# Gate tiles dealt out, logits one group later, 96 rows straight from the second layer: one change to an attention and mixture-of-experts kernel

## The chip, the cores and the metric

The kernel runs as one program on one core of a Trainium2 chip. The metric is the device time of one execution in microseconds (us), the median of several. PE (TensorE) multiplies matrices, DVE (VectorE) and ACT (ScalarE) compute elementwise, POOL (GpSimd) does both and issues indirect DMAs, SP (SyncE) issues most DMAs. "SPq" and "ACTq" in a row are the DMA queues behind SP and ACT.

## What is computed

Three stages follow one another. Attention with a bias from cumulated positive scores, on 4 x 8 heads of 576 positions and width 64:

```
scores = q k^T / 8;  cum = cumsum(max(s, 0))
scores = where(causal, -1e9, scores + min(cum_j - cum_i, 0))
x = softmax(scores) v              # as 2304 tokens x 512
h = x @ w_in                       # 512 -> 2048, float64 weights
g = h * clip(h + 3, 0, 6) / 6
x = g @ w_out                      # 2048 -> 512
logits = x @ w_gate                # 8 experts, each takes 288 tokens
for (token, e) in descending order of logits:
    assign token to e, if the token is free and e not full
out[tokens of e] = max(x[tokens of e] @ w1[e], 0) @ w2[e]    # 512 -> 1024 -> 512
```

## The kernel before

**Numbers.** Every large operand is held as two 16-bit halves (high and low), and a product is three matmuls: high by high, high by low, low by high. "Split product" below is one with the low half of its left side.

**Attention.** Pairs of heads go through three stages, in a pipeline: rows of scores, columns of scores, value products. For pair n, `prep(n)` puts q and k side by side as 16-bit halves (`kq`), and line 250 turns them by a transposing DMA into `kqT`, from which line 282 takes the scores (`sc`). For pair 0 the turn is in two parts, 4 of 9 blocks on SP and 5 on ACT; for all others it is one on SP.

**First MLP.** A decoder (`decode`, lines 500 to 512, ACT, DVE and POOL) turns the float64 weights into halves, `wih`/`wil` for w_in and `woh`/`wol` for w_out (tile `W`, the low half made by POOL at line 512); `ST["w"]` counts the loads that are decoded, 8 of w_in and then 8 of w_out, two blocks of 128 rows each. Tokens go in 9 groups of 256. `h_step` (line 551) makes two blocks of h of a group (12 matmuls of 256 columns each), g is formed by ACT, DVE (559, 571) and POOL (572). `x2_tile` (lines 593 to 595) makes the MLP's output for 128 tokens, three matmuls of 512 columns for each of 16 blocks, into a bank called "mm" of which there are two; the result `xo` is stored to DRAM (`x2d`, line 620) as two halves.

**Gate and logits.** For the first ten of 18 token tiles (groups 0 to 4) the logits come straight from x2: xo is turned by DMA (`x2T`, line 608) and multiplied by the gate (`direct_logits`). For the last eight tiles (groups 5 to 8, `DEFER`) the logits are needed before x2 is there, and come from g instead: `gates` turns the 16 blocks of w_out, high and low (`gate_turn`, line 521, two DMAs from SP per block into a buffer `wT` of which there are three), multiplies them by the gate (`gate_product`, lines 527 and 528, eight matmuls per block) to `gm`, and `logits(u)` (580, 581) takes the logits of group u as 64 small matmuls of g with gm, in an "mm" bank. For groups 5 to 8 x2 follows after all logits, in the tiles 10 to 17, beside the routing.

**Routing.** The logits give a key per token and expert (`keys`); `route(ph)` finds one expert after another by a search for its threshold (compares on DVE, counts on PE, a few values passed between them, `kst` being one), and `tail` turns the selection into 288 indices. `gather` fetches the tokens' rows from x2d (POOL, line 1115, `xg`), three DMAs of 96 rows; `tokens` turns them to `xt` (line 1123, three transposing DMAs on SP). The last two token tiles are not in DRAM when the first expert's rows are gathered; they are picked out by matmuls (`pick`, line 1220) and added to xt by DVE (1223, four additions).

**Experts.** `groups(ph)` makes `ht` (first layer, line 1132, 8 blocks of 128 rows, 288 columns) and `yt` (second layer, 4 blocks, 96 matmuls in all, 288 columns). yt stands with the features down the partitions, so `store` turns it back by matmuls with the identity (line 1163, 8 for each 96 rows), copies it (ACT, 1166) and scatters the rows to the output (POOL, line 1168).

**What sets the order.** The attention, the decoder, the MLP and the gate are Python generators (`Stream`) which a planner, `merge`, deals out: it picks the stream that is least far along, each yield giving an estimate of the time its matmuls take; a yielded condition blocks a stream until it holds, and a yielded negative number -n keeps a stream back until the planner's clock has gone n ns further (the gate's stream goes first whenever it is ready). The tile framework then schedules the instructions by priority within their dependencies, adds the semaphores, and gives buffers in turn; `high_priority` lifts a block ahead of what stands near it, and `issue_after` holds a DMA behind a given instruction. Each engine runs its own instructions in the order that comes out.

Of the kernel before, what the change touches and what calls it, by code (L numbers as in the profile page):

```python
# [23 lines left out]
HP = 20000  # L24
# [75 lines left out]
def tile_attention_moe(ctx, tc, q, k, v, s, w_in, w_out, w_gate, w1, w2, out):  # L100
# [129 lines left out]
    def prep(n):  # L230
# [18 lines left out]
        for eng, s0, s1 in ((nc.sync, 0, 9),) if n else ((nc.sync, 0, 4), (nc.scalar, 4, 9)):  # L249
            pin(eng.dma_start_transpose(out=t[:, s0:s1].rearrange("p s w x -> p (s w) x"),  # L250
                                        in_=kq[:, s0:s1].rearrange("p s w x -> p (s w x)")))
# [323 lines left out]
    def logits(u):  # L575
        p = psum.tile([128, 2, 16], F32, name="mm", tag="mm", bufs=2)
        for t in range(2):
            for f in range(FT1):
# [5 lines left out]
                                axis=AX.X, op=OP.add)  # L584

    def x2_tile(t):
        u, o = divmod(t * 128, UN)
        p = psum.tile([128, DM], F32, name="mm", tag="mm", bufs=2)
        for f in range(FT1):
            if ST["w"] < 2 * FP:  # L590
                yield from wait(lambda: ST["w"] > FP + f // 2)
# [37 lines left out]
    def mlp():  # L629
        for u in range(NU):  # L630
# [4 lines left out]
            for fp in range(HE + HX if u == 1 else 0, FP):  # L635
                yield from wait(lambda: ST["w"] > fp)
                yield from h_step(u, fp)
                if fp == FP // 2 and ("x2T", 2 * u - 1) in GT:
                    direct_logits(2 * u - 1)
                    yield 8 * 27.0  # L640
                    if "keys" in GT:
                        GT["keys"](u - 1)
            if late:
                yield -2500.0
# [15 lines left out]
            yield from wait(lambda: ST["g"])  # L660
            yield from logits(u)
            if "keys" in GT:
                GT["keys"](u)
# [16 lines left out]
    def gates():  # L680
        turned = []
        for f in range(FT1 + 2):
# [5 lines left out]
            yield -2500.0  # L688
# [438 lines left out]
    def split_product(wh, wl, x, o, kt):  # L1127
        n, last = 0, 3 * kt - 1
        p = mm_tile([128, CAP])
# [9 lines left out]
    def groups(ph):  # L1139
# [9 lines left out]
        yt = [ffn.tile([128, 2, CAP], F16, name="yt", bufs=2 * KC) for _ in range(KC)]  # L1149
        YT[ph] = yt  # L1150
        for d in range(KC):
            p = split_product(w2h, w2l, lambda hl, f: ht[:, hl, f, :], d, FMT)
            e = nc.scalar.activation(yt[d][:, 0], p, AF.Copy)  # L1153
            nc.vector.tensor_tensor(yt[d][:, 1], p, yt[d][:, 0], op=OP.subtract)
            yield e.ins

    def store(ph):
        yt = YT.pop(ph)
        for j in range(3):
# [7 lines left out]
            nc.gpsimd.memset(spacer, 0.0)  # L1167
            st_ = nc.gpsimd.indirect_dma_start(out, bass.IndirectOffsetOnAxis(ap=IDX[ph][:, j:j + 1], axis=0), yo, None)  # L1168
            for o in SCAT:
                tc.declare_no_dep(st_.ins, o.ins, reason="different rows")  # L1170
            SCAT.append(st_)

    for t in range(NT - DEFER, NT):
        merge([Stream(x2_tile(t), 1.0)])
# [28 lines left out]
    for i in range(4):  # L1203
        for c in range(4):
            convert(0, i, c, GT["xo", NT - DEFER + 3 + i])
        sp = load(1, i - 1, sp) if i else load(0, 3, sp)
    g_stack.close()
    ffn = ctx.enter_context(tc.tile_pool(name="ffn", bufs=1))
    with tc.high_priority(offset=HP):
        sp = tokens(0, sp)  # L1210
# [31 lines left out]
    store(E8 - 1)  # L1242
# [28 lines left out]
```

## Time and profile before

| | |
|---|---|
| median of 3 runs | 926.36 us (924.86 to 927.57) |
| the profiled execution | 926.86 us |
| its span, first to last instruction | 924.7 us |
| PE busy | 824.6 us (89% of the span) |
| weight loads of PE (beside its matmuls) | 588.6 us (64%) |
| DVE, POOL, ACT busy | 554.3, 467.4, 373.3 us |
| mean granted clock of PE | 0.958 of full speed |

The page gives each engine's busy time for the whole span and for 40 equal slices of it. The timeline lists an engine's instructions in order of time; a wait is the idle time of an engine just ahead of an instruction, with the instruction or DMA that came last of those it needed. [...] In the timeline of the kernel before, the first h product comes at 119 us; from there to 440 us attention, h and x2 of the groups run side by side. The gate's tiles stand between 448 and 500 us, the logits and h of groups 5 to 8 between 502 and 583, x2 of the last tiles and the search for the first experts until some 685, the experts' products behind that, with the rest of the search beside them.

### The profile page before, as it was taken

The numbers are of one execution on the slowest core, as the hardware profiler recorded it, in microseconds if no ns is written. First come the engines' busy times: TensorE is split into PE (matmuls) and PEld (weight loads), VectorE is DVE, ScalarE is ACT, GpSimd is POOL, SyncE is SP. The second block draws the span as 40 slices with busy tenths as digits, with TensorE's granted clock in tenths as the row PEclk, the third lists the DMA queues.
The fourth block names the chain that finished last, engine by engine and source line by source line (L and its number), as shares of the span: only waits on it lengthen the run. The fifth ranks groups of instructions, "written<-read, shape, count | busy, mean of one in ns | idle before, by whom it ended". The sixth has DMA issues, their size and how long they took to land. (4 is left out here: it accounts for less than half of the span.)

```text
span 924.7 us, 21475 instructions
## 1 busy us (share of the span) xinstructions
PE 824.6 (89%) x8561; PEld 588.6 (64%) x8561; DVE 554.3 (60%) x1698; ACT 373.3 (40%) x704; POOL 467.4 (51%) x485
## 2 busy tenths in 40 slices
PE   1576779778899999999888999999989999999996
PEld 0354557545567857759567988444457777778885
DVE  5979879967535645513625455675777887772211
ACT  1666766656425444443111222002223554355641
POOL 1455766854433544644412433003437786787951
PEclk9976789999799999999998999999999999999998
DMA  6987999667723445221473000032346775776820
GB/s 150 213 186 186 230 184 268 134 148 182 145 52 70 96 103 102 42 51 40 89 122 57 2 1 1 13 125 104 129 129 180 189 216 167 208 214 205 194 77 26
DMA packets 225700, 116.31 MB, mean 126 GB/s; under 512 B 202272, under 2 KB 202272, under 8 KB 225600
## 3 DMA queue, kind: packets, MB, share of 16 engines
q1 hardware_dynamic: 220576, 105.01, 48.1%
q0 software_dynamic: 3072, 9.44, 3.2%
q8 instruction: 67, 1.10, 0.5%
q10 hardware_dynamic: 1952, 0.49, 0.3%
q14 instruction: 33, 0.27, 0.1%
HBM read 69.30 MB, written 9.96 MB: 86 GB/s over the span
## 5 line engine op out<-in xcount | busy, mean ns | idle before, releaser
L551 PE MATMUL mm<-xT,W 128*128 128x256 f16 (+3 forms) x2304 | 205.3, 248 | 5.4 <-DVE g L559 3.8
L1110 POOL TENSOR_TENSOR W<-stg,W 128x512 bf16<-128x512 f32 x128 | 144.7, 1157 | 92.6 <-ACT W L1108 91.8
L551 PEld LDWEIGHTS <-W 128*128 128x128 f16 (+1 forms) x2304 | 177.3, 99 | 19.2 <-issue 4.8
L1132 PEld LDWEIGHTS <-W 128*128 128x128 f16 (+1 forms) x1536 | 144.2, 98 | 38.8 <-issue 4.0
L365 POOL TENSOR_TENSOR eh<-e,eh 128x512 f16<-128x512 f32 (+1 forms) x100 | 104.6, 1061 | 102.0 <-ACT eh L363 95.2
L572 POOL TENSOR_TENSOR g<-g,g 128x512 f16<-128x512 f32 x72 | 85.3, 1185 | 134.7 <-DVE g L571 119.2
L282 PE MATMUL sc<-kqT 96*128 96x64 f16 (+10 forms) x480 | 102.1, 295 | 40.3 <-DMA kqT<-kq 22.4
L594 PE MATMUL mm<-W,g 128*128 128x512 bf16 x288 | 110.4, 383 | 6.4 <-POOL W L512 6.3
L593 PE MATMUL mm<-W,g 128*128 128x512 f16 x288 | 110.0, 385 | 5.7 <-DVE g L559 4.2
L595 PE MATMUL mm<-W,g 128*128 128x512 f16 x288 | 110.9, 385 | 0.0
L1132 PE MATMUL mm<-xt,W 128*128 128x288 f16 x768 | 103.0, 286 | 2.6 <-DVE ht L1146 2.2
L1132 PE MATMUL mm<-ht,W 128*128 128x288 f16 x768 | 102.7, 286 | 0.0
L557 ACT ACTIVATE r<-mm,three 128x512 f32<-128x512 f32 x72 | 49.4, 686 | 128.3 <-PE mm L551 123.0
L282 PEld LDWEIGHTS <-kqT 101*128 101x128 f16 (+5 forms) x768 | 52.9, 107 | 72.2 <-DMA kqT<-kq 26.4
L296 DVE TENSOR_REDUCE mx<-sc 128x1 f32<-128x384 f32 (+2 forms) x144 | 70.1, 512 | 40.3 <-PE sc L293 26.0
L362 ACT ACTIVATE e<-sc 128x512 f32<-128x512 f32 (+1 forms) x112 | 59.0, 538 | 56.2 <-PE sc L350 50.7
L559 DVE SCALAR_TENSOR_TENSOR g<-r,mm 128x512 f32<-128x512 f32 x72 | 49.2, 684 | 48.8 <-ACT r L557 48.2
L1108 ACT ACTIVATE W<-stg 128x512 f16<-128x512 f32 x128 | 75.5, 622 | 0.0
L363 ACT ACTIVATE eh<-e 128x512 f16<-128x512 f32 (+1 forms) x112 | 60.7, 570 | 22.1 <-PE pv L419 20.2
L417 PE MATMUL pv<-v,eh 128*128 128x65 f16 (+1 forms) x480 | 67.7, 203 | 1.9 <-DVE x L430 1.9
L419 PE MATMUL pv<-v,eh 128*128 128x65 f16 (+1 forms) x480 | 66.5, 199 | 2.0 <-POOL eh L365 2.0
L418 PE MATMUL pv<-v,eh 128*128 128x64 f16 (+1 forms) x480 | 66.9, 201 | 1.0 <-DVE v L220 1.0
(221 smaller groups left out, 1343.3 us busy)
## 6 DMA issues: line engine op xcount, KB each, us to landing
stg<-in_moe_w_dram SPq DMA_DIRECT2D x32, 1024.0 KB
raw<-in_moe_w_in_dram SPq DMA_DIRECT2D x8, 1024.0 KB
raw<-in_moe_w_out_dram SPq DMA_DIRECT2D x8, 1024.0 KB
x2d<-xo SPq DMA_DIRECT2D x18, 256.0 KB
ldq<-in_q_dram SPq DMA_DIRECT2D x32, 128.0 KB
ldk<-in_k_dram SPq DMA_DIRECT2D x32, 128.0 KB
ldv<-in_v_dram SPq DMA_DIRECT2D x32, 128.0 KB
ldq<-in_q_dram SPq DMA_DIRECT2D x16, 32.0 KB
```

Of the source, the lines that this page charges most:

```text
L282: nc.tensor.matmul(o, x[0:kq], y[0:kq], start=start, stop=stop)
L296: nc.vector.tensor_reduce(o, x, axis=AX.X, op=OP.max)
L365: eng.tensor_tensor(t[:, 1], e, t[:, 0], op=OP.subtract)
L417: nc.tensor.matmul(oj[:, 0:65], e[0], vv[:, 0:65], start=a, stop=False)
L551: nc.tensor.matmul(p[:, f, at:at + w], wsl(wt, ft)[:, c * 128:(c + 1) * 128], XT[b][:, c, hl, i:i + w], start=(n == 0), stop=(n == 3 * KC ...
L572: nc.gpsimd.tensor_tensor(g[:, 1].rearrange("p f x -> p (f x)"), g32, g[:, 0].rearrange("p f x -> p (f x)"), op=OP.subtract)
L593: nc.tensor.matmul(p, g[:, 0], wsl(woh, f), start=(f == 0), stop=False)
L594: nc.tensor.matmul(p, g[:, 0], wsl(wol, f), start=False, stop=False)
L595: nc.tensor.matmul(p, g[:, 1], wsl(woh, f), start=False, stop=(f == FT1 - 1))
L1108: nc.scalar.activation(h, x, AF.Copy)
L1110: nc.gpsimd.tensor_tensor(l, x, h, op=OP.subtract)
L1132: nc.tensor.matmul(p, wt[:, c, o * 128:(o + 1) * 128], x(hl, c), start=(n == 0), stop=(n == last))
```

## The change

Seven edits stand in one diff.

1. The second part of pair 0's transpose is issued by SP (`nc.sync`) instead of ACT.
2. `x2_tile` waits, while w_out is being decoded, until one load more is counted (at most all but one) before the planner may deal out the three matmuls of a block.
3. `gates` yields -4000 instead of -2500 between blocks: the planner keeps the stream back longer.
4. `logits(u)` is no longer made right after group u's h: the group's number goes into a list, `owed`, and the oldest of the list is taken within the h of a later group (after the block pairs 2 and 5 of groups 7 and 8, if one is owed and the gate is done), the rest at the end, behind the first two steps of x2 of tile 10 (`GT["begun"]`).
5. The logits are summed in a bank of the tag "tp" (name `lgp`) instead of "mm". `keys(u)` is called from `logits`.
6. `tokens(0)`, the three transposes of the first expert's rows, is called in the loop that loads and converts the first weights, ahead of the load of the second expert's third block, instead of after the loop.
7. For the last expert the second layer's product is made as before for 192 of the 288 columns only (`w`). The last 96 rows come from `store_last`: ht of these rows as the left side, w2 as the right, 24 matmuls of 512 columns, so that the result stands with the tokens down the partitions and needs no turning back. `store` of the first 192 rows is placed behind the ninth of these matmuls. `store` itself is cut in two (`put` is its scatter).

The core of the diff:

```diff
@@ prep(n)
-        for eng, s0, s1 in ((nc.sync, 0, 9),) if n else ((nc.sync, 0, 4), (nc.scalar, 4, 9)):
+        for eng, s0, s1 in ((nc.sync, 0, 9),) if n else ((nc.sync, 0, 4), (nc.sync, 4, 9)):
@@ logits(u)
-        p = psum.tile([128, 2, 16], F32, name="mm", tag="mm", bufs=2)
+        p = psum.tile([128, 2, 16], F32, name="lgp", tag="tp", bufs=TPB)
...
+        if "keys" in GT:
+            GT["keys"](u)
@@ x2_tile(t)
-                yield from wait(lambda: ST["w"] > FP + f // 2)
+                yield from wait(lambda: ST["w"] > min(FP + f // 2 + 1, 2 * FP - 1))
@@ mlp()
+        owed = []
         for u in range(NU):
...
+                if u > NU - DEFER // 2 + 1 and fp % 3 == 2 and owed:
+                    yield from wait(lambda: ST["g"])
+                    yield from logits(owed.pop(0))
             if late:
-                yield -2500.0
+                owed.append(u)
...
-            yield from wait(lambda: ST["g"])
-            yield from logits(u)
-            if "keys" in GT:
-                GT["keys"](u)
+        GT["begun"] = x2_tile(NT - DEFER)
+        for _ in range(2):
+            yield next(GT["begun"])
+        while owed:
+            yield from logits(owed.pop(0))
@@ gates()
-            yield -2500.0
+            yield -4000.0
@@ groups(ph), second layer
+        w = CAP if ph + 1 < E8 else CAP - RW
-            p = split_product(w2h, w2l, lambda hl, f: ht[:, hl, f, :], d, FMT)
+            p = split_product(w2h, w2l, lambda hl, f: ht[:, hl, f, 0:w], d, FMT)
@@ new
+    def store_last(ph):
+        w2h, w2l = (x.rearrange("p (k f) -> p k f", f=DM) for x in W[ph, 1])
+        p = mm_tile([RW, DM])
+        n, last = 0, 3 * FMT - 1
+        for f in range(FMT):
+            for wt, hl in ((w2h, 0), (w2h, 1), (w2l, 0)):
+                nc.tensor.matmul(p, HT[0][:, hl, f, CAP - RW:], wt[:, f], start=(n == 0), stop=(n == last))
+                n += 1
+            if f == 2:
+                store(ph, (0, 1))
+        yo = ffn.tile([RW, DM], F32, name="yo", bufs=3)
+        nc.scalar.activation(yo, p, AF.Copy, scale=1.0 / (6.0 * SC))
+        put(ph, 2, yo)
@@ first expert's loads
     for i in range(4):
         for c in range(4):
             convert(0, i, c, GT["xo", NT - DEFER + 3 + i])
+        if i == 3:
+            with tc.high_priority(offset=HP):
+                sp = tokens(0, sp)
         sp = load(1, i - 1, sp) if i else load(0, 3, sp)
...
-    with tc.high_priority(offset=HP):
-        sp = tokens(0, sp)
```

What the edits move on the engines is seen in the order of the instructions. In these rows a number behind a name is its buffer, and "x3" stands for three alike in a row.

**The start.** SP at the start, before (`raw` are loads of the float64 weights, `ldq` and `ldk` of q and k; the part of 15 blocks stands on ACT):

```order
L486 DMA raw<-in_moe_w_in_dram 128x4x256
L142 DMA ldq<-in_q_dram 128x4x64 x2
L250 DMA_TRANSPOSE kqT<-kq_103 128x12x128
L143 DMA ldq<-in_q_dram 128x1x64
L142 DMA ldk<-in_k_dram 128x4x64 x2
L143 DMA ldk<-in_k_dram 128x1x64
L486 DMA raw<-in_moe_w_in_dram 128x4x256 x2
L250 DMA_TRANSPOSE kqT<-kq_103 128x27x128
```
and after:

```order
L486 DMA raw<-in_moe_w_in_dram 128x4x256
L142 DMA ldq<-in_q_dram 128x4x64 x2
L250 DMA_TRANSPOSE kqT<-kq_103 128x12x128
L250 DMA_TRANSPOSE kqT<-kq_103 128x15x128
L143 DMA ldq<-in_q_dram 128x1x64
L142 DMA ldk<-in_k_dram 128x4x64 x2
L143 DMA ldk<-in_k_dram 128x1x64
L486 DMA raw<-in_moe_w_in_dram 128x4x256 x2
L250 DMA_TRANSPOSE kqT<-kq_103 128x27x128
L332 DMA_TRANSPOSE qB<-qb_97 128x9x128
```
The 15 blocks stand right behind the 12, ahead of the loads of pair 1's q and k, and `qB` of pair 1 behind its kqT. On PE, ACT and POOL the order of the instructions is dealt anew up to the first h product; behind that, until the gates, it differs at one spot only, where edit 2 moves the last three of a run of x2 matmuls (593 to 595) of the first token tile behind four value products.

**Gates and logits.** SP between 448 and 500 us, before (`wT` the transposes of w_out, `x2d` the stores of x2, `x2T` the turn for the direct logits):

```order
L521 DMA_TRANSPOSE wT<-W 128x4x128 x3
L620 DMA x2d<-none 128x1024 x2
L521 DMA_TRANSPOSE wT<-W 128x4x128 x9
L620 DMA x2d<-xo 128x1024
L608 DMA_TRANSPOSE x2T<-xo 128x8x128
L521 DMA_TRANSPOSE wT<-W 128x4x128 x8
L620 DMA x2d<-xo 128x1024
L608 DMA_TRANSPOSE x2T<-xo 128x8x128
L521 DMA_TRANSPOSE wT<-W 128x4x128 x12
```
and after:

```order
L521 DMA_TRANSPOSE wT<-W 128x4x128 x3
L622 DMA x2d<-none 128x1024 x2
L521 DMA_TRANSPOSE wT<-W 128x4x128 x5
L622 DMA x2d<-xo 128x1024
L610 DMA_TRANSPOSE x2T<-xo 128x8x128
L521 DMA_TRANSPOSE wT<-W 128x4x128 x4
L622 DMA x2d<-xo 128x1024
L610 DMA_TRANSPOSE x2T<-xo 128x8x128
L521 DMA_TRANSPOSE wT<-W 128x4x128 x20
```
The stores and turns of token tiles 8 and 9 stand ahead of the last 24 and 20 transposes, where they stood ahead of 20 and 12. Between two gate tiles on PE stand now 21 matmuls of x2, or 48 of h and more, where there were none to 12; only tiles 12 to 15 stand close, with 12, 3, 3 and 3 matmuls of h between them. PE within the logits of group 7, before (line 551 is h of the next group, 580 and 581 the logits):

```order
L551 LDWEIGHTS W
L551 MATMUL mm<-xT,W 128x256
L551 LDWEIGHTS W
L551 MATMUL mm<-xT,W 128x256
L580 LDWEIGHTS g
L580 MATMUL mm<-gm,g 128x16
L551 LDWEIGHTS W
L551 MATMUL mm<-xT,W 128x256
```
and where the logits of a group begin after the change:

```order
L551 LDWEIGHTS W
L551 MATMUL mm<-xT,W 128x256
L551 LDWEIGHTS W
L551 MATMUL mm<-xT,W 128x256
L580 LDWEIGHTS g
L580 MATMUL lgp<-gm,g 128x16
L581 LDWEIGHTS g
L581 MATMUL lgp<-gm,g 128x8
```
Before, matmuls of h are put between the logits of groups 6 and 7; after, the 64 of a group stand unbroken behind h of a later one.

**Tokens.** SP where the first expert's tokens are turned (`stg` are loads of expert weights, 1 MB each), before:

```order
L620 DMA x2d<-xo 128x1024
L1093 ISA
L1093 DMA stg<-in_moe_w_dram 128x2x1024
L620 DMA x2d<-xo 128x1024
L1096 ISA
L1096 DMA stg<-in_moe_w_dram 128x4x512
L1123 DMA_TRANSPOSE xt<-xg 128x8x96 x3
L620 DMA x2d<-xo 128x1024
```
and after:

```order
L1100 ISA
L1100 DMA stg<-in_moe_w_dram 128x2x1024
L622 DMA x2d<-xo 128x1024
L1100 ISA
L1100 DMA stg<-in_moe_w_dram 128x2x1024
L1130 DMA_TRANSPOSE xt<-xg 128x8x96 x3
L1103 ISA
L1103 DMA stg<-in_moe_w_dram 128x4x512
L622 DMA x2d<-xo 128x1024 x2
```
The three turns of xg stand one load of 1 MB earlier. DVE at the additions of the picked rows, before (lines 986 to 1003 end one expert's search):

```order
L990 TENSOR_TENSOR og<-ohu,ra 128x18x8 x2
L993 TENSOR_SCALAR ra<-rb 128x18
L994 TENSOR_TENSOR ra<-ra,un 128x18
L1000 TENSOR_REDUCE rb<-tot 128x16
L996 TENSOR_TENSOR ra<-ra,un 128x18
L1002 TENSOR_TENSOR rb<-rb,cap 128x8
L1223 TENSOR_TENSOR xt<-xt,pick 128x2x256 x4
L1003 TENSOR_TENSOR rb<-rb,prio 128x8
```
and after (lines 988 to 937 are within the second expert's search, 931 to 937 lead to kst):

```order
L988 TENSOR_SCALAR d<-rb 128x18
L990 TENSOR_TENSOR rb<-d,ra 128x18
L922 TENSOR_TENSOR cmp<-rb,th_4096_6850 128x576
L1054 TENSOR_TENSOR ohr<-slotr,rb 128x576
L1252 TENSOR_TENSOR xt<-xt,pick 128x2x256 x2
L931 TENSOR_TENSOR rest<-cap,cnt 32x8
L1057 TENSOR_TENSOR rb<-rb,part 128x54
L933 TENSOR_TENSOR f<-cnt,rest 32x8
L1058 TENSOR_TENSOR rb<-rb,m 128x54
L603 TENSOR_TENSOR xo<-mm,xo 128x512
L937 TENSOR_REDUCE km<-kst 128x1
```
Two of the four additions stand now in the middle of the second expert's search, behind the one-hot compare `ohr`; all four stood behind that search.

## Rows read from the trace of the kernel before

**Rows 1.** Page, part 2: PE's busy tenths in 40 slices of 23.1 us.
```profile
PE   1576779778899999999888999999989999999996
```

**Rows 2.** Windows: us, busy of PE, PEld, DVE, ACT, POOL (instructions), PEclk, DMA, GB/s.
```profile
450.00:500.00 50.00, 41.61 (x407) 29.47 (x408) 23.75 (x123) 6.69 (x10) 13.70 (x44) 1.00 0.61 115
```

**Rows 3.** Timeline of the start: start, duration, engine, line, operation, [wait <- releaser].
```profile
11.80 1.42 ACTq L250 DMA_TRANSPOSE kqT<-kq  x1
16.20 1.56 SPq L250 DMA_TRANSPOSE kqT<-kq  x1
20.04 0.50 PE L282 MATMUL sc<-kqT 99*128 99x384 f16 x1 [11.51 <-DMA kqT<-kq]
118.77 0.37 PE L551 MATMUL mm<-xT,W 128*128 128x256 f16 x1 [1.66 <-DVE mag L509]
```

**Rows 4.** Waits of PE, 178 to 236 us: total, times, longest, us.
```profile
PE mm L594 <- POOL W L512: 6.3, 6, 1.8
```

**Rows 5.** Waits of PE, 449 to 502 us.
```profile
PE tp L528 <- DMA wT<-W: 5.5, 6, 1.5
PE mm L580 <- DVE gm L690: 1.6, 1, 1.6
PE tp L527 <- issue: 1.2, 1, 1.2
PE tp L527 <- DMA wT<-W: 1.1, 1, 1.1
```

**Rows 6.** Line 521's transposes (ns min/median/max), and the timeline's last such wait.
```profile
L521 SPq DMA_TRANSPOSE wT<-W x32: 1188/1265/2481, 448.4 to 497.1; - x32
...
499.85 0.18 PE L528 MATMUL tp<-wgh,wT 128*128 128x8 f16 x1 [1.39 <-DMA wT<-W]
```

**Rows 7.** Waits of PE, 502 to 583 us.
```profile
PE mm L581 <- POOL g L572: 1.8, 4, 0.6
PE mm L551 <- DVE g L559: 1.4, 2, 0.7
PE mm L593 <- DVE g L559: 0.7, 1, 0.7
```

**Rows 8.** Windows of two stretches at the low clock, and timeline of PE.
```profile
501.62:508.45 6.83, 6.48 (x103) 6.17 (x103) 3.29 (x22) 0.00 (x0) 1.16 (x1) 0.50 0.01 2
556.24:559.65 3.41, 3.41 (x21) 2.43 (x19) 2.10 (x13) 0.00 (x0) 0.00 (x0) 0.50 0.00 0
...
531.79 20.25 PE L551 MATMUL mm<-xT,W 128*128 128x256 f16 x184
556.20 21.91 PE L551 MATMUL mm<-xT,W 128*128 128x256 f16 x184
```

**Rows 9.** Timeline and landing times of the token gathers, 660 to 690 us.
```profile
663.06 0.92 POOL L1115 DMA_INDIRECT xg<-x2d,idx  x1 [0.30 <-issue]
DMA to landing us min/median/max: 5.5/6.0/6.4
665.92 0.74 DVE L1047 TENSOR_TENSOR ohr<-slotr,rb 128x576 f16<-128x576 f16 x1
673.65 5.45 SPq L1123 DMA_TRANSPOSE xt<-xg  x3
681.23 2.50 DVE L1223 TENSOR_TENSOR xt<-xt,pick 128x512 f16<-128x512 f16 x4 [1.39 <-DMA xt<-xg]
681.97 0.38 PE L1220 MATMUL pick<-lastsel,xo 128*128 128x256 f16 x2 [1.12 <-DVE xt L1223]
```

**Rows 10.** Timeline of the end, 895 to 925 us.
```profile
902.37 11.92 PE L1132 MATMUL mm<-ht,W 128*128 128x288 f16 x96
916.28 0.61 PE L1163 MATMUL y<-ident,yt 128*96 128x128 f16 x8 [0.68 <-ACT yo L1166]
916.97 0.59 ACT L1166 ACTIVATE yo<-y 96x512 f32<-96x512 f32 x1 [0.26 <-ACT yo L1166]
918.95 0.92 POOL L1168 DMA_INDIRECT out_dram<-yo,idx  x1 [0.30 <-issue]
```

More of the change, by code (lines that the diff above doesn't have):

```diff
@@ L1128, in split_product @@
         n, last = 0, 3 * kt - 1
-        p = mm_tile([128, CAP])
+        p = mm_tile([128, x(0, 0).shape[-1]])
         for c in range(kt):
@@ L1148, in groups @@
         w2h, w2l = (x.rearrange("p (k f) -> p k f", f=DM) for x in W[ph, 1])
-        yt = [ffn.tile([128, 2, CAP], F16, name="yt", bufs=2 * KC) for _ in range(KC)]
+        w = CAP if ph + 1 < E8 else CAP - RW
+        yt = [ffn.tile([128, 2, CAP], F16, name="yt", bufs=2 * KC)[:, :, 0:w] for _ in range(KC)]
         YT[ph] = yt
         for d in range(KC):
-            p = split_product(w2h, w2l, lambda hl, f: ht[:, hl, f, :], d, FMT)
+            p = split_product(w2h, w2l, lambda hl, f: ht[:, hl, f, 0:w], d, FMT)
             e = nc.scalar.activation(yt[d][:, 0], p, AF.Copy)
@@ L1155, in groups, with put, store @@
             yield e.ins
-    def store(ph):
+        HT[0] = ht
+    HT = {}
+    def put(ph, j, yo):
+        nc.gpsimd.memset(spacer, 0.0)
+        st_ = nc.gpsimd.indirect_dma_start(out, bass.IndirectOffsetOnAxis(ap=IDX[ph][:, j:j + 1], axis=0), yo, None)
+        for o in SCAT:
+            tc.declare_no_dep(st_.ins, o.ins, reason="different rows")
+        SCAT.append(st_)
+    def store(ph, js=(0, 1, 2)):
         yt = YT.pop(ph)
-        for j in range(3):
+        for j in js:
             p = cpsum.tile([RW, DM], F32, name="y", tag="y", bufs=YB)
@@ L1166, in store @@
             nc.scalar.activation(yo, p, AF.Copy, scale=1.0 / (6.0 * SC))
[L1167 to L1171, printed above, removed]
+            put(ph, j, yo)
+    def store_last(ph):
[11 more added lines that the diff above has]
+        put(ph, 2, yo)
     for t in range(NT - DEFER, NT):
-        merge([Stream(x2_tile(t), 1.0)])
+        merge([Stream(GT["begun"] if t == NT - DEFER else x2_tile(t), 1.0)])
     with tc.high_priority(offset=HP):
@@ L1241, in tile_attention_moe @@
                 store(ph - 1)
-    store(E8 - 1)
+    store_last(E8 - 1)
 _INS = ["q", "k", "v", "s", "moe_w_in", "moe_w_out", "moe2_w_gate", "moe2_w1", "moe2_w2"]
```

## Prediction

> **What bounds the kernel now.** I read the 40 slices first, to see where TensorE (PE) is not full: the first ten slices (to some 230 us) stand at 1 to 9 tenths and mostly below 8, then come nines, with dips to 8 at the gate and the logits (slices 20 to 22) and where the tokens are turned (slice 30), and a last slice of 6 [rows 1]. In the stretch 450 to 500 us PE is busy 41.6 of 50 us [rows 2]. So from 230 us on PE sets the pace, and an idle us of PE there is a us of the run; before 230 us chains through DMA, VectorE (DVE) and PE share the pace, and a us saved may be lost again. The second view is the waits of PE in the stretches that the change touches, the third the granted clock, the fourth the timeline at the token transposes and at the end. The sum is made against the profiled execution, 926.86 us (span 924.7 and 2.2 around it); the median of the three runs is 0.5 us lower.
>
> **Start: second half of pair 0's transpose moved from ACT's queue to SP's.** ACT issues its part at 11.80, SP its own only at 16.20, and PE's first score matmul waits for it until 20.04 [rows 3]. All inputs of SP's half were there when ACT issued; what SP waits for is the other transpose. On one queue both go out behind one another: the first at 11.80, the second 1.42 (ACT's issue, [rows 3]) later, so PE may begin up to 16.20 - 11.80 = 4.40 us earlier. On SP the issue stands ahead of the loads of pair 1, which had to wait behind the late transpose too. On the other side, if SP's wait stayed, SP would lose the 1.42. What of it is left when the first layer's h product begins (118.77, [rows 3]) is not in the trace, since DVE and DMA chains lie between, and the order of some 800 matmuls there is dealt anew. Ends: +4.4 gain, -1.4; I take **2.5**, nearer the upper end, because that wait opens the chain.
> [...]
>
> **The x2 product planned one load behind: 0.** PE waits 6.3 us for the low half of the output matrix between 178 and 236 us [rows 4]. The order shows that three matmuls of the first token tile move behind four value products and nothing else does; the waits sit at later tiles, whose places are the same. Ends: 0 and 6.3.
>
> **Gate tiles spread: 8.2.** Removed are PE's waits for the transposed tiles (5.5 and 1.1), for the first one (1.2) and for the gate's product in VectorE (1.6) [rows 5]: 9.4. After, between two gate tiles stand 21 matmuls of x2 or 48 of h at 109 ns (20.25 us for 184, [rows 8]), about 5 us, where a pair of transposes costs two issues of 1.27 [rows 6] and lands 1.5 after (last issue from 497.1 to 498.4, used at 499.85, [rows 6]): 4.0. So the tiles come in time, but not the last ones: gate tiles 12 to 15 stand together, with only 12 + 3 + 3 + 3 h matmuls between them (2.3 us) and three gate tiles (0.5), and tile 15's transposes may start only when tile 12 frees its buffer. Wait there: 4.0 - 2.8 = 1.2. The gate's VectorE wait is covered by ten h matmuls (1.1 us) of the 1.6, the rest by rounding of this estimate. Ends: 6.5 to 9.4.
>
> **Logits a group behind, in another bank: 3.5.** Of the waits 1.8, 1.4 and 0.7 [rows 7], 3.9 in all, the two at the split products of groups 6 and 7 and the one at 5 go, since the g tiles are a group old and the logits no longer take an "mm" bank in which the h product needs room. The last group has nothing after it: 6 matmuls of x2 ahead, then again a wait on GpSimd's g of at most 0.6; I keep 0.4. Ends: 3.0 to 3.9. Early x2 matmuls only change their place.
>
> **Clock: 4.1.** [...] Ahead of the first PE had mostly waited for transposes, ahead of the second it had run 16-column products between the logits' waits. The second made the same 184 matmuls 21.91 in place of 20.25 [rows 8]: 1.7. The first is twice as long but holds logits too: 1.7 to 3.3, I take 2.4. Both causes shrink, so I take all of it; ends: 0 and 5.
>
> **Token transposes ahead of a weight load: a loss of 3.3.** Now PE waits 1.12 at 681.97 [rows 9], since the three transposes go out at 673.65, behind the load of 1 MB. After, they go out when the gathers have landed: the third is issued at 663.06 and lands 6.0 later (median) [rows 9], 669.1, plus its issue of 1.27 and 1.5 to 2.1 (2.1: end of the three issues 679.10 to 681.23, [rows 9]): 671.9 to 672.5. That takes the 1.12 away. But the order also moves VectorE's first two additions to xt from behind the second route's search into its middle, right behind the one-hot compare of line 1047 that now ends at 666.66 [rows 9]. VectorE runs in order: it would stand there from 667.4 to about 672, then add for 1.3 (half of the 2.5 that the four adds make), and then form the counts that PE waits for ("kst"). On PE eight x2 matmuls (1.7 us) lie between the count and kst; PE comes to it at about 669.3 and gets it at about 673.7: 4.4 lost, 1.1 won. Ends: 1.1 won (additions find xt in place) and 5.5 lost.
>
> **End: 1.5.** The second layer's 96 matmuls take 11.92, 122 ns for 288 columns [rows 10], 0.425 per column: 192 columns make 81.6 ns and save 3.9. 24 direct ones of 512 columns add 24 x 217 ns = 5.2; 8 transposing ones (0.61, [rows 10]) go. PE ends 0.7 later, but the last rows then need only the copy. PE: 902.37 + 7.8 + 9 x 0.217 + 1.1 + 15 x 0.217 and 0.2 to land = 916.7; copy 0.59 [rows 10], then 0.3 to GpSimd, which is free, having issued the other two: the last store goes at 917.6 in place of 918.95 [rows 10]. Between 1.0 and 2.0; what follows the store is the same.
>
> **Sum.** 2.5 + 0 + 8.2 + 3.5 + 4.1 - 3.3 + 1.5 = 16.5: 926.86 - 16.5 = 910.4, less 0.5 for the median: **910.0 us**.
>
> **Rivals.**
> - The tokens land before VectorE comes to the additions. For it: the gathers' issue follows the x2 stores and may move earlier; against: 6.0 to land is the median of all six here. 1.1 won in place of 3.3 lost: 905.6. Chance 0.20.
> - The clock falls once more, at the last gate tiles or at the new wait on kst. For it: it fell behind such a stretch at 501.62; against: the wait of 1.1 at 681 was followed by no fall. 4.1 lost: 914.1. Chance 0.18.
> - The start wins nothing, as ACT's issue now lies on SP (1.42) ahead of the loads, and VectorE's chain absorbs the rest: 910.0 + 2.5 + 0.7 = 913.2 with half of the 1.42. [...] For it: PE is idle anyway in the first 230 us; against: the 4.40 at its head. Chance 0.14.
> - The x2 plan does what its words say, and the 6.3 goes: 903.7. The order speaks against it. Chance 0.03.
> - Slower: the new order of the first 118.77 us. One delay, as at SP, where the transposes of stage n now stand ahead of the loads of stage n + 2: each stage then starts late by what its loads lose, and they add up over some eight pairs. The first h product comes at 118.77 now; if it came later than 118.77 + 2.5 + 16.5, about 138 us, the run would be slower; that is 2.4 us lost per pair. At 3 us per pair: 932. For it: PE's clock and chains are fragile there; against: most pairs' rows stand as before. Chance 0.05.
> - Forecast: 0.40.
>
> **How the numbers follow.** Range 902 to 920: it holds the forecast, the first four rivals, clock and start together (917.3) and with them the gate at its lower end (1.7 more); left out are the slower case and the mixtures that add the lower ends of tokens and clock. About 0.3% (2.8 us) is what a measurement can tell from no change. Faster by more: all but the slower case and 0.04 for mixtures that eat the gain, 0.91; within: 0.04; slower: 0.05.
>
> **What would show it.** In the changed profile: PE's first score product at 16 rather than 20; the first h product 2 to 3 us earlier; PE's waits for wT near 1 us; no wait within the logits but the last; granted clock 1.00 between 480 and 600; a PE wait of about 4 us at kst in the second route, named by VectorE and behind it a token DMA; the last scatter 1.5 us nearer to PE's last product. Wrong it would be made by a first h product that isn't earlier, or by waits for wT that stay above 4 us.

## The result, and the profile of the changed kernel

The changed kernel takes **914.68 us** (median of 4 runs, 913.52 to 915.35), the kernel before beside it 926.97: a ratio of 0.987, 95% interval 0.985 to 0.989. Run again later it took 913.14 against 926.02, 0.986 (0.983 to 0.989). Forecast were 910.0 and a range of 902 to 920: the direction is as told, and the gain is 12.3 us in place of 16.5.

Where the 12 us lie is read from four events on PE's timeline: the last value product of the attention, the first count step of the search (`kst`), the first product of the last expert's second layer, and the end of the span. They cut the program into a start (attention, decoder, first groups), a gate stretch (gate, logits, rest of h, some x2), a token stretch (search, picked rows, experts) and an end. In us, from the profiled execution of each kernel, start of event to start of event (the runs are told of below):

| kernel | start | gate stretch | token stretch | end |
|---|---|---|---|---|
| before | 439.2 | 154.6 | 308.5 | 22.3 |
| changed | 438.7 | 138.2 | 314.7 | 21.1 |
| changed, again | 439.9 | 138.7 | 311.6 | 21.1 |
| start edit alone | 441.4 | 152.6 | 306.6 | 22.6 |
| token edit alone | 438.1 | 152.9 | 306.6 | 22.3 |
| gate and logits alone | 435.5 | 139.6 | 312.3 | 22.3 |
| start undone | 437.0 | 139.7 | 310.9 | 20.8 |
| x2 wait and end undone | 437.3 | 138.7 | 309.6 | 22.6 |
| tokens undone | 444.2 | 138.7 | 312.2 | 21.1 |
| spacing undone | 438.6 | 141.4 | 316.8 | 21.1 |
| putting off undone | 439.7 | 148.9 | 314.0 | 21.1 |
| additions moved | 440.5 | 138.7 | 309.5 | 21.1 |
| additions moved, prio in PSUM | 437.1 | 137.0 | 310.8 | 21.1 |
| combined version | 439.3 | 138.7 | 307.2 | 20.8 |

So the gate stretch gave 16.5 (and 15.9 when run again), the end 1.2, the start 0.6 or -0.7, and the token stretch lost 6.1 or 3.1. The kernel before's own execution is on the long side in two columns: the kernels that share its order there have 152.6 and 152.9 in the gate stretch (start edit alone, token edit alone) and 306.6 in the token stretch (start edit alone). Against these the gate stretch gave some 14 to 15 us, and the token stretch lost 5 to 8. These are single executions. Where kernels of this table share their order, they differ by up to 7 us in the start (437.1 to 444.2), by 2.7 in the gate stretch (137.0 to 139.7) and by 7 in the token stretch (309.6 to 316.8); smaller differences in a column prove nothing by themselves.

The page of the changed kernel, PE's busy tenths and the granted clock, in tenths of full speed, in 40 slices (beside [rows 1]; here 22.8 us each): the dip at the gate, slices 20 to 22, is gone, and the one at the tokens, now 29 and 30, is still there.

```profile
PE   2477679788899999999999999999889999989996
PEclk9977679999899999999999999999889999999999
```
PE's waits in the changed kernel, 449 to 523 us (total, times, longest; beside [rows 5], 9.4 us in four rows):

```profile
PE lgp L580 <- DVE gm L697: 0.9, 1, 0.9
PE tp L528 <- DMA wT<-W: 0.8, 1, 0.8
```
The same view from 523 to 567 us (beside [rows 7]):

```profile
PE lgp L581 <- POOL g L572: 0.6, 1, 0.6
```
Of the 13.3 us of [rows 5, 7] 2.3 us are left: the transpose of one of the last gate tiles (0.8) and the last group's g (0.6), which the prediction kept at 1.2 and 0.4, and the gate's product in VectorE (0.9), which it put at nothing.

Why the tiles waited before is plain from PE's order. Between two gate tiles of the kernel before stand 12 matmuls of x2 or 24 of h, and none only ahead of the last tile ("none to 12" in the section on the change is wrong). Either makes 2.6 us, at 217 ns for one of x2 and 110 for one of h, where the prediction works out 4.0 us for a pair of transposes. After the change it is 4 us and more, except ahead of the last tiles.

Timeline of the changed kernel at the tokens (beside [rows 9]): start, duration, engine, line, what, and the wait with what ended it.

```profile
645.13 0.92 POOL L1122 DMA_INDIRECT xg<-x2d,idx  x1 [0.30 <-issue]
648.04 3.93 SPq L1130 DMA_TRANSPOSE xt<-xg  x3
649.50 0.74 DVE L1054 TENSOR_TENSOR ohr<-slotr,rb 128x576 f16<-128x576 f16 x1
653.48 1.28 DVE L1252 TENSOR_TENSOR xt<-xt,pick 128x512 f16<-128x512 f16 x2 [3.23 <-DMA xt<-xg]
654.99 0.16 DVE L933 TENSOR_TENSOR f<-cnt,rest 32x8 f16<-32x8 f32 x1
655.20 0.16 PE L935 MATMUL kst<-f,sn 32*128 32x8 f16 x1 [2.62 <-DVE f L933]
```
This is the wait that the prediction built from the order: VectorE ends the compare at 650.2, stands before the addition until the tokens land at 653.5, then adds for 1.3 us, and only then forms f, for which PE waits 2.62 us at kst. (The search that the prediction and the order's rows call the second is the third: two searches of seven steps stand before it. Nothing hangs on that.)

### The profile page after: what moved, and what is told of

The parts are those of the page before. It is cut to its first block, busy times and chain, and to the rows that moved or that the text cites. A ratio compares the mean times of both kernels' runs of the same rounds, so it can differ in the third digit from the quotient of the medians.

```text
span 912.6 us, 21502 instructions
## 1 busy us (share of the span) xinstructions
PE 824.8 (90%) x8577; PEld 591.3 (65%) x8577; DVE 555.5 (61%) x1698; ACT 372.4 (41%) x704; POOL 467.3 (51%) x485
## 5 line engine op out<-in xcount | busy, mean ns | idle before, releaser
L551 PE MATMUL mm<-xT,W 128*128 128x256 f16 (+3 forms) x2304 | 203.0, 246 | 2.6 <-DVE g L559 2.6
L282 PE MATMUL sc<-kqT 96*128 96x64 f16 (+10 forms) x480 | 100.2, 292 | 36.8 <-DMA kqT<-kq 16.8
L1139 PE MATMUL mm<-ht,W 128*128 128x288 f16 (+1 forms) x768 | 98.8, 281 | 0.0
L417 PE MATMUL pv<-v,eh 128*128 128x65 f16 (+1 forms) x480 | 70.3, 208 | 6.9 <-DVE x L430 6.0
L419 PE MATMUL pv<-v,eh 128*128 128x65 f16 (+1 forms) x480 | 69.5, 205 | 1.1 <-POOL eh L365 1.1
L418 PE MATMUL pv<-v,eh 128*128 128x64 f16 (+1 forms) x480 | 69.9, 207 | 0.5 <-DVE v L220 0.5
```

What stands on the lines that cost most here:

```text
L282: nc.tensor.matmul(o, x[0:kq], y[0:kq], start=start, stop=stop)
L417: nc.tensor.matmul(oj[:, 0:65], e[0], vv[:, 0:65], start=a, stop=False)
L551: nc.tensor.matmul(p[:, f, at:at + w], wsl(wt, ft)[:, c * 128:(c + 1) * 128], XT[b][:, c, hl, i:i + w], start=(n == 0), stop=(n == 3 * KC ...
L1139: nc.tensor.matmul(p, wt[:, c, o * 128:(o + 1) * 128], x(hl, c), start=(n == 0), stop=(n == last))
```

## The experiments

Three kernels are the kernel before with some of the edits, one is the changed kernel itself, the others are the changed one with something undone or moved. Beside the three batches of runs the kernel before took 923.01 us (start undone, x2 and end undone, tokens undone, additions moved), 926.02 (changed again, prio in PSUM, the two of experiment 3) and 922.79 (the three on the kernel before, the combined version); so the ratios to it are compared, not the times.

> The changed kernel itself once more, as the measure for the three that run beside it on this chip. Expected: 0.987 of the kernel before. What it tells besides is how much the first 230 us move between executions of one and the same order: the two theories on the start differ by 2.5 us, and the run with late tokens lost 5.5 us there with PE's order unchanged.

It is the second row of the changed kernel in the table.

**1. The start, undone and alone.** Undone: `(nc.scalar, 4, 9)` for `(nc.sync, 4, 9)` in the changed kernel.

> The changed kernel with one edit undone: the second part of pair 0's transpose again on ACT's queue; PE's order of the first 118 us is then that of the kernel before. Theory from the two traces: the start's lead of 4.2 us is gone by 134 us and worth 0.6 at most later, so this kernel takes 914.7 to 915.3. Rival, the prediction's term: 2.5 us are kept, so 917.2. [...]

909.07 us, ratio 0.984 (0.981 to 0.987), against 0.987 and 0.986 for the changed kernel. It was expected no faster than the changed kernel; the intervals touch, so undoing the edit costs nothing, and whether it gains is open. Alone:

```
-        for eng, s0, s1 in ((nc.sync, 0, 9),) if n else ((nc.sync, 0, 4), (nc.scalar, 4, 9)):
+        for eng, s0, s1 in ((nc.sync, 0, 9),) if n else ((nc.sync, 0, 4), (nc.sync, 4, 9)):
```

> The kernel before with the first edit alone: the second part of pair 0's transpose on SP's queue. Prediction's term: 2.5 us faster than the kernel before beside it. Theory from the ten traces so far: PE's first score comes 4.2 us earlier, but by 134 us the lead is gone and the last value product comes as before (439.2, within the 2 us by which executions differ there): 0, within 1.5 us either way.

923.47 us, ratio **1.001 (0.998 to 1.004)**: nothing; the 2.5 us of the forecast would be 0.997. Its timeline at the head (beside [rows 3]):

```profile
11.77 3.70 SPq L250 DMA_TRANSPOSE kqT<-kq  x2
15.86 0.50 PE L282 MATMUL sc<-kqT 99*128 99x384 f16 x1 [7.33 <-DMA kqT<-kq]
```
And its first h product:

```profile
122.27 0.63 PE L551 MATMUL mm<-xT,W 128*128 128x256 f16 x2
```
Both transposes leave back to back and PE's first score starts 4.18 us earlier (15.86 for 20.04), as the prediction said. But the first h product, 118.77 before, comes at 122.27 here and 121.14 in the changed kernel: the lead stands between 3 and 8 us over most of the first 240 score matmuls and is gone by the 300th, between 107 and 131 us. There the matmuls' order was dealt anew: 791 of PE's matmuls stand ahead of the first of h, in place of 730. And PE waits there for the row maxima of VectorE (8.0 us between 85 and 135 us in the changed kernel, 2.1 before). What of the loss is the order and what the chain of DMA and VectorE was not taken apart.

**2. The x2 wait and the end undone.** Diff: `ST["w"] > FP + f // 2` in x2_tile, `w = CAP` in groups, `store(E8 - 1)` for `store_last(E8 - 1)`.

> The changed kernel with two edits undone that lie far apart in time: the planner's wait of x2 for one load more, and the last 96 rows straight from the second layer. Theory: x2 is worth 0 (PE's waits for the low half of w_out stay at 6 to 7 us between 178 and 236 us), and the end is worth 1.2, to be read between the start of the last second layer and the end of the span: 915.9. Rival for x2: the plan does what it says and hid something, then waits of PE there differ by over 2 us. Rival for the end: the copy and the scatter behind it set the end either way: 914.7.

910.16 us, ratio 0.986 (0.983 to 0.988). PE's waits for the low half of w_out between 178 and 236 us in the changed kernel, beside the 6.3 of [rows 4]:

```profile
PE mm L596 <- POOL W L512: 6.8, 6, 1.7
```
And in this one:

```profile
PE mm L596 <- POOL W L512: 6.8, 6, 1.7
```
The x2 edit does nothing to these waits, as the order said. The end takes 22.6 in place of 21.1 us: 1.5, as the prediction had it. The ratio is that of the changed kernel, so the 1.5 us are seen in their stretch and not in the whole time.

**3. The spacing and the putting off, each undone.** `yield -2500.0` for `yield -4000.0` in gates; and in mlp

```
-                if u > NU - DEFER // 2 + 1 and fp % 3 == 2 and owed:
-                    yield from wait(lambda: ST["g"])
-                    yield from logits(owed.pop(0))
             if late:
-                owed.append(u)
+                yield -2500.0
+                yield from wait(lambda: ST["g"])
+                yield from logits(u)
```

> The changed kernel with the gate tiles as close as before (-2500 in place of -4000). Theory, from the prediction: PE waits again for wT, 8 to 9 us of waits, and the clock falls behind them: 8 to 11 us over the changed kernel beside it. Rival: since the logits are put off, the waits' time is given back later (h products do not run out), so the spacing by itself is worth less than 4 us.

> The changed kernel with the logits of a group again right behind its h (still in their own bank, the gate tiles spread). Theory, from the prediction: the waits on g come back (3 to 4 us) and with them a fall of the clock (1.7 to 2.4): 4 to 6 us over the changed kernel beside it. Rival: the separate bank was what counted, and the order in time costs under 2 us.

The first took 919.99 us (0.994, 0.991 to 0.997), the second 929.35 (1.004, 1.001 to 1.007), the changed kernel beside them 913.14. In the gate stretch alone that is +2.7 and **+10.2** us against it. Of the first one's 7 us the rest lies in the token stretch, where VectorE, ScalarE, GpSimd and SyncE have the changed kernel's order: the granted clock is 0.50 there for 6.8 and for 3.4 us, as in the changed kernel's first execution, and not in its second. Where the rest of the second one's 16 us lies is open: its profiled execution, 925.50 us, is among the fastest of ten. My split of the 16 us among the edits was wrong both times. Waits of PE with the tiles close, 440 to 600 us:

```profile
PE tp L528 <- DMA wT<-W: 2.3, 3, 1.2
PE tp L527 <- issue: 1.2, 1, 1.2
PE tp L527 <- DMA wT<-W: 1.1, 1, 1.1
```
And with the logits at once, 440 to 590 us:

```profile
PE tp L527 <- DMA wT<-W: 3.8, 5, 2.1
PE tp L528 <- DMA wT<-W: 2.6, 5, 0.8
PE lgp L581 <- POOL g L572: 1.4, 3, 0.5
```
The windows of the stretch where these lie (us; busy time and instructions of PE, PEld, DVE, ACT, POOL; granted clock; share and GB/s of DMA):

```profile
490.00:508.00 18.00, 11.53 (x152) 8.26 (x150) 3.36 (x13) 1.37 (x2) 2.31 (x2) 0.67 0.42 89
508.00:512.00 4.00, 4.00 (x93) 3.95 (x92) 1.48 (x6) 0.00 (x0) 1.16 (x1) 0.76 0.00 0
```
With the logits at once, the stream of h stops behind group 5, since the logits want the gate; the last nine gate tiles then have few matmuls to lie between (4 to 21 of h from one to the next, where the changed kernel has 48 to 96 up to tile 12), however far apart the planner wants them. PE waits 6.4 us for transposes, and the granted clock of that stretch is 0.67. With the logits put off and the tiles close, the waits of the first tiles come back (2.3 + 1.2 + 1.1), but those of the last ones and of the gate's product do not, and the granted clock is 1.00 from 440 to 580 us: h goes on. So putting the logits off carries most of the gain, and spreading the tiles is only possible with it. Both kernels keep the logits' own bank; what it gives alone was not run.

**4. Gate and logits alone**, on the kernel before.

> The kernel before with the gate and logits edits alone (spacing, putting off, own bank); start, x2 wait, tokens and end as before. Prediction's terms gate, logits and clock: 15.8 us. Theory: from the last value product to the first kst 138 to 139 us in place of 154.6, so 16 us there; of that some 6 us are given back at the last expert's choice, since the order of the search then is that of the runs with late tokens (VectorE's operation of 8 columns waits for GpSimd's run): 10 us faster than the kernel before beside it, with that operation near 5 us. Rival: the place of the additions, not the order of the search, brings that wait; then it is absent and the gain 16.

914.56 us, ratio 0.992 (0.989 to 0.996): 8.2 us under the kernel before beside it, where 10 were expected. The gate stretch is 139.6, 15.0 less than before and 13 less than in the start and the token edit alone, and part of it is given back at the last expert's choice, see 6.

**5. The tokens undone, with the additions moved, and alone.** Undone, `tokens(0, sp)` stands behind the loop again. Moved, with the instruction kept of each step of the search:

```
+            KMI.append(nc.vector.tensor_reduce(km, p, axis=AX.X, op=OP.min).ins)
...
+                with behind(KMI[20]):
+                    nc.vector.tensor_tensor(x, x, p, op=OP.add)
```

> The changed kernel with one edit undone: the three transposes of the first expert's tokens stand again behind the load of 1 MB, and VectorE's four additions to xt behind the third expert's search. My theory: the early tokens cost 7.3 us in the changed kernel, 2.6 of it PE's wait for kst and the rest two falls of the clock that idle PE brings on; this kernel then takes about 907.5, and the granted clock is 1.00 in the 20 us around the picked rows, as in the kernel before. Rival 1: the clock falls there whatever stands in the order (PE runs x2 and small products in turn), so only the wait goes: 912. Rival 2: the transposes gain what they were moved for and something else took the 7 us: 914.7 or more.

> The changed kernel, the transposes of the tokens early as in the change, but VectorE's four additions to xt queued behind the last step of the third expert's search, so that VectorE never stands at its head for the token DMA. Theory: the loss is VectorE's order alone, so the kst wait and the falls of the clock go, and the 1.1 us that PE waited for xt in the kernel before goes too: about 906.5, 1 us under the run with late tokens. Rival: the early transposes themselves (DMA against the loads) are what delays: then it stays at 912 to 914.7.

Undone it took 915.67 us (0.990, 0.987 to 0.994), with the additions behind the search 912.05 (0.988, 0.985 to 0.990); against 0.987 and 0.986 for the changed kernel neither is faster, so the expected 907.5 and 906.5 were wrong. Yet up to the first expert the theory holds: from the first kst to the first second-layer product they take 105.3 and 103.3 us, the kernel before 105.5, the changed one 111.8 and 107.7; there is no wait at kst in either, and the granted clock is 1.00 from 640 to 690 us. The loss moved: behind it both wait 4.8 us at one place that the changed kernel does not wait at (6). Alone, on the kernel before:

> The kernel before with the token edit alone. The order that comes out puts VectorE's first additions one step of the search later than in the changed kernel, and ten x2 products and four picked ones ahead of the kst that waits for them. Theory: not the early transposes cost, but the place of the additions; here the tokens have landed when VectorE comes to them, PE does not wait over 1 us at kst, the clock stays at 1.00, and the time is within 2 us of the kernel before, rather under it. Rival, the prediction's price as such: 3 us slower, with a wait at kst.

921.67 us, ratio **0.999 (0.997 to 1.001)**. VectorE waits for the tokens here too, but ten x2 matmuls lie on PE ahead of the kst:

```profile
668.74 1.29 DVE L1224 TENSOR_TENSOR xt<-xt,pick 128x512 f16<-128x512 f16 x2 [2.41 <-DMA xt<-xg]
```
PE has no wait at kst; just ahead of it it waits 0.95 us at the picks for VectorE's xo. By themselves the early transposes neither cost nor gain; the place that the scheduler gave the additions in the changed kernel costs PE the wait.

**6. The wait at the last expert.** Rows of the run with the additions moved, POOL, VectorE and PE:

```profile
800.55 8.93 POOL L1118 TENSOR_TENSOR W<-stg,W 128x512 bf16<-128x512 f32 x8
804.52 4.99 DVE L964 SCALAR_TENSOR_TENSOR rb<-om,prio 128x8 f32<-128x8 f32 x1
810.38 0.20 PE L949 MATMUL pre<-m,before 128*128 128x18 f16 x1 [4.75 <-DVE m L1042]
```
An operation of 8 columns takes 4.99 us. It reads two tiles in SBUF (`om`, `prio`), and it stands within GpSimd's run of conversions that PE needs only later. The same 4.99 appears in the run with gate and logits alone, and in that with tokens undone PE waits 4.8 us at the same place; in the changed kernel and the kernel before the operation falls where GpSimd issues its scatters and converts nothing, and takes 0.18. One change tells whether it is the operand: prio copied to PSUM once, and read there.

```
+    priop = near([E8], "pp", bank="b")
+    nc.vector.tensor_copy(priop, prio)
-            nc.vector.scalar_tensor_tensor(left, om, 0.0, prio, op0=OP.is_equal, op1=OP.mult)
+            nc.vector.scalar_tensor_tensor(left, om, 0.0, priop, op0=OP.is_equal, op1=OP.mult)
```

> The run add_late (token transposes early, VectorE's additions behind the third expert's search) with one small thing more: the operand prio of the last expert's choice is read from PSUM instead of SBUF. In add_late that operation of 8 columns took 4.99 us, ending 0.03 us after GpSimd's run of six conversions; PE waited 4.75 us for it. Theory: VectorE's operation with both inputs in SBUF has to wait until GpSimd's run ends, and early tokens with late additions are better by what they gave at the tokens: then this wait is gone and the run is 5 to 6 us under add_late (912.05), some 4 us under the changed kernel beside it. Rival: the long operation is something else (loading of code, the semaphore behind it): then it is again near 5 us, and the time that of add_late.

The same rows of GpSimd and VectorE with prio in PSUM:

```profile
802.51 8.95 POOL L1120 TENSOR_TENSOR W<-stg,W 128x512 bf16<-128x512 f32 x8
806.89 0.16 DVE L966 SCALAR_TENSOR_TENSOR rb<-om,rb 128x8 f32<-128x8 f32 x1
```
In the midst of such a run it takes 0.16 for 4.99: shown, the operand in SBUF was the cause. (GpSimd's run has eight conversions, not the six of the expectation.) The time is 912.43 (0.987, 0.982 to 0.993; single runs from 907.73 to 918.80), not the 906 expected. In the profiled execution, the one of 907.73, the wait of 4.75 is gone, but the token stretch is not shorter: 310.8 us for 309.5. PE waits for VectorE at other places, between 690 us and the end:

```profile
PE mm L1142 <- DVE ht L1156: 3.3, 4, 1.1
PE kst L938 <- DVE f L936: 1.4, 2, 1.2
PE cnt L931 <- DVE cmp L927: 0.8, 1, 0.8
```
The run without the copy has none of these there. The order of VectorE, ScalarE, GpSimd and SyncE is the same but for the copy and the operand; why these waits come is open.

**7. The combined version**: the start as before, the additions behind the third of the four last steps (`KMI[19]`), so that the rest of the search keeps the changed kernel's order.

> The changed kernel with pair 0's second part on ACT's queue as before, and VectorE's first four additions queued behind the third of the four steps of the search's second level (the transposes of the tokens stay early). The order of the rest of the search is that of the changed kernel. Theory: no wait at kst, no fall of the clock between 640 and 690 us, no long operation at the last expert: from the first kst to the first second-layer product 104 us in place of 107 to 112, and 4 to 6 us under the changed kernel: 0.980 of the kernel before. Rival: the loss only changes its place, as it did in add_late; then it is within 1.5 us of the changed kernel, 0.986.

**906.22 us**, ratio 0.984 (0.979 to 0.988), 16.6 under the kernel before beside it; 0.980 was expected. PE's waits between 640 and 690 us of this version (total, times, longest):

```profile
PE mm L1140 <- DVE xt L1254: 1.2, 2, 0.7
PE pick L1250 <- ACT xo L602: 0.7, 1, 0.7
PE pick L1250 <- DVE xo L603: 0.4, 1, 0.4
```
The window of the same stretch, columns as above:

```profile
640.00:690.00 50.00, 47.67 (x374) 27.65 (x373) 38.50 (x143) 13.12 (x27) 26.12 (x25) 0.97 0.49 148
```
And of the changed kernel:

```profile
640.00:690.00 50.00, 45.05 (x321) 24.90 (x318) 33.78 (x125) 11.73 (x24) 23.25 (x23) 0.90 0.44 127
```
The wait at kst is gone, VectorE makes all four additions without waiting, and the last expert's operation takes 0.17. The clock still falls once, to 0.50 from 668.9 us for 3.4 us, behind the short waits of the rows above. The kernel before waits as long there in all and has no fall, and in the changed kernel's second execution it is 1.00 over the whole window. From the first kst to the first second-layer product it is 106.1 us, more than the 104 expected and less than the changed kernel's 111.8 and 107.7; the token stretch is 307.2 us, 4.4 and 7.5 under the two executions of the changed kernel. The intervals of the two ratios overlap, so that it is faster than the changed kernel is likely but not proven. And the changed kernel with only the start undone (1) has the same ratio, 0.984; so no whole time shows that pinning the additions gains, only the wait and the stretch do (307.2 us, where all six executions with the wait at kst have 309.6 to 316.8). Nor does the stretch fall below the 306.6 us of the kernels with the old gate and logits: pinned or not, the early transposes are nowhere seen to gain.

## Why the prediction was right, and where its sizes were off

- **Gate, logits and clock, 15.8 forecast: 16.5 and 15.9 measured** (some 14 to 15 against the two kernels that share the old order).
  - *Waits.* PE's waits of over 0.25 us between 440 us and the end of the logits add up to 13.7 before and 2.2 after: 11.5, for the 8.2 + 3.5 of the sum. Of the remainders the gate's product (0.9) was put at nothing; the other two are 1.4 in place of 1.6.
  - *Faster matmuls.* The other 5.0 are matmuls that run faster, for the 4.1 of the clock. Not all of its falls went: the granted clock was 0.50 of full speed for 10.2 us in this stretch before (the two stretches of [rows 8], the first and the second of the prediction's term), and is for 3.4 us in both executions of the changed kernel, so the "1.00 between 480 and 600" did not come. By the 1.7 us that the prediction reads for 3.4 us at the low clock, the 6.8 us less are worth 3.4, an estimate. Another 1.4 the sum had not: the 256 logits, waits of over 0.25 us aside, take 7.9 us before and 6.5 after. One stands 25 to 27 ns behind the other in the median of either; what went are pauses of 0.15 to 0.35 us, one or two in a group.
  - *Which edit.* Wrong was which edit gives what: without the putting off, the spacing is worth much less than the 8.2 of its step.

The window of the fall that is left, behind the wait for the gate's product:

```profile
523.70:527.00 3.30, 3.30 (x52) 2.64 (x50) 1.41 (x7) 0.69 (x1) 0.00 (x0) 0.52 0.00 0
```
- **Start, 2.5 forecast: nothing.** The head of the chain was right (4.2 for the 4.40), the step "nearer the upper end, because that wait opens the chain" was not. By the prediction's own sign the term is wrong: the first h product is not 2 to 3 us earlier but 2.4 later (121.14 for 118.77). The rival "the start wins nothing" held, for its second reason: the lead was absorbed in the stretch before 230 us (gone by the 300th score matmul, experiment 1). The issuing engine did matter to the transposes, by 4.2 us (first score at 15.86 for 20.04); it was the work behind that made nothing of it. (In the slower rival, a first h product at which the other gains are used up is 118.77 - 2.5 + 16.5 = 132.8 us, not 138; nothing hangs on it.)
- **x2, 0 forecast: 0.** The order was enough to see it.
- **Tokens, -3.3 forecast: -6.1 and -3.1.**
  - *The wait at kst* was sized 4.4 and measured 2.62 and 2.81. Counted from the issue of the third gather (645.13), PE came to kst after 7.5 us, not 6.2, and got it after 10.1, not 10.6. The 6.0 us to land, which the prediction puts on the third gather, belong to the first two, the only ones with a landing in that trace (6.4 and 5.5); in the eight runs that record it the third lands after 3.8 to 4.2.
  - *The 1.1 us won at the picks* did not come: PE's waits at the picks and at the first products behind them add up to 2.5 us before and 2.3 after (the rows of experiment 7, the same in the changed kernel).
  - *The clock.* In the profiled execution it fell behind the wait at kst (2.62 us; 0.58 from 655.3 to 663.3), the rival "the clock falls once more at the new wait"; in the second execution, with the same order and the same wait (2.81 us), it did not (1.00 from 657.2 to 663.3). A second fall, behind the picks (0.63 from 672.5 to 677), comes in the combined version too (0.50 from 668.9 us for 3.4), which has no wait at kst.
  - *Luck.* The loss was forecast against the kernel before. Against the changed kernel with the tokens undone the edit loses nothing (0.987 for 0.990), because there PE waits 4.8 us at the last expert, which no term foresaw.

Windows of the first execution behind the wait at kst and behind the picks, where the granted clock stands third from the end:

```profile
655.30:663.30 8.00, 8.00 (x47) 4.24 (x47) 3.83 (x13) 0.00 (x0) 0.00 (x0) 0.58 0.46 166
672.50:677.00 4.50, 3.85 (x22) 2.39 (x20) 2.84 (x17) 0.77 (x2) 1.58 (x2) 0.63 0.22 69
```
And in the second:

```profile
657.20:663.30 6.10, 5.94 (x51) 3.35 (x52) 4.33 (x15) 0.00 (x0) 0.00 (x0) 1.00 0.69 218
672.50:677.00 4.50, 4.17 (x36) 3.19 (x35) 3.93 (x25) 2.96 (x7) 2.42 (x3) 1.00 0.24 62
```
- **End, 1.5 forecast: 1.2 in the span, 1.5 to the last scatter** (from the last second layer's first product to the scatter's issue 16.58 before, 15.11 after); what follows the scatter took 0.3 longer.

In sum, for the profiled execution, forecast less measured: start 2.5 - 0.6, gate stretch 15.8 - 16.5, tokens 6.1 - 3.3 lost more, end 1.5 - 1.2: 1.9 - 0.7 + 2.8 + 0.3 = 4.3 us, up to rounding the distance from 16.5 to the 12.1 by which the spans differ. In the second execution the tokens lose no more than forecast and the start's part is 3.2. The terms that failed are the start, taken near its upper end, and the clock behind kst, taken at nothing.

## What to carry to other kernels

A lead at the head of a long pipeline (4.18 us here) is worth nothing until it is seen at the last event of the stretch; look for it there before it enters a sum. When transposes are spread to be hidden, look first for the stream that must lie between them, since it may itself be blocked on their result (with the logits at once PE waited 6.4 us). And an operation made ready earlier can be scheduled earlier, ahead of work on which another engine waits: here VectorE stood 3.23 us before the additions, with f behind them, and PE waited 2.62 us at kst for f. Pinning the operation took the wait away and kept the transfer early. Whether the early transfer then gains anything has still to be seen in the stretch; here it did not.

## What the runs showed of the hardware

A VectorE operation with two inputs in SBUF, among GpSimd's conversions back to back, took 4.99 us for 8 columns, alike in two kernels, and ended where GpSimd's run ended: with the additions moved at 809.51 (804.52 + 4.99) for 809.48 (800.55 + 8.93), with gate and logits alone at 807.52 (802.53 + 4.99) for 807.49 (798.55 + 8.94). With one input in PSUM, among such conversions too, it took 0.16, and with both in SBUF but no conversion beside it 0.18. At 1.12 us a conversion (8.93 / 8), VectorE waited out not only the conversion that was running but four more behind it.

The granted clock is not a function of the order alone. At one wait at kst it fell to 0.50 in four executions (waits of 2.62, 2.49, 3.03 and 2.53 us: changed, start undone, spacing undone, putting off undone) and stayed at 1.00 behind it in two (2.81 and 2.54: changed again, x2 wait and end undone). And the first 440 us of one and the same order differed by up to 7 us between executions (437.1 to 444.2, seven executions of six kernels), which is more than most edits of this change moved.
